# Pooled attention with a SoLU mixture layer on one core: the first four tiles' score maxima subtracted by TensorE, small scale steps merged, the order searched anew

## The chip, the cores and the metric

The kernel runs on one core of one Trainium2 chip, in one launch. The metric is device time in microseconds (us), as the median of the runs shown. The engines are called as in the profile: PE (TensorE; PEld is its weight load), DVE (VectorE), ACT (ScalarE), POOL (GpSimd) and SP, which here only issues DMAs.

## The reference

```python
def _attn_ref(q, k, v):                    # (8, 8, 576, 64) each
    k_p = k.reshape(B, H, 72, 8, D).mean(axis=3)
    v_p = v.reshape(B, H, 72, 8, D).mean(axis=3)
    scores = scale * np.matmul(q, k_p.transpose(0, 1, 3, 2))
    scores = scores - np.max(scores, axis=-1, keepdims=True)
    attn = np.exp(scores)
    attn = attn / (np.sum(attn, axis=-1, keepdims=True) + 1e-09)
    return np.matmul(attn, v_p)
def _moe_ref(x, w_in, w_out, g_ln):        # x (4608, 512), w_in (512, 1024), w_out (1024, 512)
    h = x @ w_in
    e = np.exp(h - np.max(h, axis=-1, keepdims=True))
    solu = h * (e / (np.sum(e, axis=-1, keepdims=True) + 1e-09))
    ln = (solu - mean(solu)) / np.sqrt(var(solu) + 1e-06) * g_ln
    return ln @ w_out
```

## The kernel before, in words

The 4,608 tokens are 36 tiles of 128. The batches go in pairs: four tiles of the even batch, one mixed tile that holds the last 64 tokens of both, four tiles of the odd batch. Each number that TensorE multiplies is held as two float16 parts, "hi" and "lo", so that a product takes three passes: hi by hi, hi by lo and lo by hi. The scale of such a pair is a power of two that is found on the chip: a maximum (`a_max`, L424), a spread over the partitions by PE (`a_par`, L470 and L480), a second maximum (`a_all`, L483) and three small DVE steps (`a_scale`, L489 to L499).

A tile goes through these steps (function, engine): `q_hi` ACT, `q_lo` DVE, a transpose of q by DMA (by PE for tile 0), `scores` PE, `s_max` DVE (L919), `s_sub` DVE (L922), `s_exp` ACT (L929), `e_sum`, `e_rec`, `e_mul` DVE, `e_hi` ACT, `e_lo` POOL, a transpose (by DMA; `e_Tp`, `e_Tc` by PE and ACT for tile 0), `av` PE (L998), `x_hi` ACT (L1007), `x_lo` DVE (L1011), `mm1` in three parts of 16 matmuls on PE (tile `hp`), `h_max`, `z_scale`, `z_mul` DVE, `h_exp`, `z_cen`, `z_hi`, `z_var` ACT, `z_lo` POOL, two transposes `z_T` by DMA, `mm2` in three parts on PE (tile `op`), `o_evac` ACT (L1150), `o_store`. Line 272 is the helper `mm`, which cuts a matmul with 128 weight columns into two with 64 each.

Ahead of the first `mm1` the weights are made ready. They arrive as 64-bit numbers, in four pieces of 1,024 KB for each matrix (wi 0 to 3, wo 0 to 3). `w_exp` and `w_sgn` (ACT), `w_shift` and `w_tail` (DVE) and `w_mul` (POOL) make float32 of a piece, `w_bnd` (PE), `w_rmax`, `w_all` and `wi_scale` or `wo_scale` (DVE, L704 and L756) its scale, `w_hi` (ACT, L788 and L791) the hi part, `w_res` (PE, L809 and L812) with `w_lo` (ACT, L823), or `w_lod` (DVE, L817), the lo part. K and V of batch 0 are pooled on PE with an identity in float32 (`pool_pe`, L405, evicted by `pool_ev`, L416), those of the others on POOL (`pool_kv`, L395).

Two things set the order. The buffers in PSUM: `ps_s` and `ps_x` have one buffer each (scores and K's transpose share the first, attention outputs, spreads and `v_rep` the second), `ps_h` has two (`hp`, the residues of the weights, PE's transposes). And the table `ORDER`: every operation has a number in it, the program emits them in that order, and each engine works off its queue in the order of these numbers; the durations and due times beside each `op` call do not enter the emitted program.

```python
    def op(eng, dur, t, fn, *args, r=(), w=(), u=(), after=()):
        ...
        ops.append((ORDER[name][count[name]], fn, args))
    ...
        for _, fn, args in sorted(ops, key=lambda o: o[0]):
            fn(*args)
```

By the table, PE's queue ahead of the first `mm1` ends with: `w_res` wo 1, `a_par` for K of batch 1, `e_Tp` 0, `v_rep` 0, `scores` 3, `w_res` wo 0, `av` 0. ACT's queue from `w_exp` wo 3 to the first `x_hi` holds three `w_hi` of wi among its work.

## Time and profile before

| | before |
|---|---|
| median of 3 runs | 493.37 us (492.62 to 495.02) |
| the profiled execution | 493.96 us |
| its span, first to last instruction | 492.2 us |
| PE busy | 464.2 us, 94% of the span |
| DVE busy | 371.7 us, 76% |
| ACT busy | 332.2 us, 67% |
| POOL busy | 305.8 us, 62% |
| DMA | 88.92 MB, mean 181 GB/s |

The profiled execution is 1.76 us longer than its span, and 0.59 us longer than the median. Times in the rows below are in us from the span's start. A busy share is a mean over stages that differ: the first 65 us hold no `mm1` at all, and in the last 20 us PE has only `mm2` left.

### The profile page before, as it was taken

The numbers are of one execution on the slowest core, as the hardware profiler recorded it, in microseconds if no ns is written. First come the engines' busy times: TensorE is split into PE (matmuls) and PEld (weight loads), VectorE is DVE, ScalarE is ACT, GpSimd is POOL, SyncE is SP. The second block draws the span as 40 slices with busy tenths as digits, with TensorE's granted clock in tenths as the row PEclk, the third lists the DMA queues.
The fourth block names the chain that finished last, engine by engine and source line by source line (L and its number), as shares of the span: only waits on it lengthen the run. The fifth ranks groups of instructions, "written<-read, shape, count | busy, mean of one in ns | idle before, by whom it ended". The sixth has DMA issues, their size and how long they took to land.

```text
span 492.2 us, 14712 instructions
## 1 busy us (share of the span) xinstructions
PE 464.2 (94%) x5976; PEld 301.0 (61%) x5976; DVE 371.7 (76%) x808; ACT 332.2 (67%) x521; POOL 305.8 (62%) x520
## 2 busy tenths in 40 slices
...
GB/s 301 359 309 197 160 103 188 182 215 165 216 213 216 201 217 128 247 178 209 189 174 166 179 200 204 188 143 174 212 215 171 114 156 125 116 102 136 55 117 87
DMA packets 197940, 88.92 MB, mean 181 GB/s; under 512 B 174312, under 2 KB 182512, under 8 KB 197360
## 3 DMA queue, kind: packets, MB, share of 16 engines
...
q14 instruction: 21, 0.17, 0.1%
...
## 4 chain that ended last, share of the span: by engine, by line
PE 63%; DVE 10%; POOL 10%; DMA 7%; ACT 4%; issue 3%; SPq 2%; POOLq 0%; ACTq 0%; DVEq 0%
PE op L272 27%; PE hp L272 26%; PE xp L998 4%; PE sc L272 3%; POOL vr L395 2%; DMA wir<-in_moe_w_in_dram 2%; DMA zT<-z 2%; DMA vr<-in_v_dram 2%; POOL kr L395 2%; POOL z L1092 2%; PE vrps L405 1%; DVE z L1072 1%; DVE m L1040 1%; POOL kp L395 1%; PE res_wo L809 1%
## 5 line engine op out<-in xcount | busy, mean ns | idle before, releaser
L272 PE MATMUL hp<-wi,xT 128*64 128x512 f16 x1728 | 197.7, 379 | 1.0 <-ACT xT L1007 0.9
L272 PE MATMUL op<-wo,zT 128*64 128x512 f16 x1728 | 197.7, 379 | 0.8 <-DMA zT<-z 0.6
L272 PEld LDWEIGHTS <-xT 128*64 128x64 f16 x1728 | 110.2, 110 | 70.4 <-ACT xT L1007 1.4
L272 PEld LDWEIGHTS <-zT 128*64 128x64 f16 x1728 | 111.3, 110 | 67.0 <-DMA zT<-z 1.1
L1092 POOL TENSOR_TENSOR z<-z,z 128x512 f16<-128x512 f32 x71 | 82.8, 1175 | 56.9 <-ACT z L1086 55.5
L1040 DVE TENSOR_REDUCE m<-hp 128x1 f32<-128x1024 f32 x36 | 43.9, 1218 | 27.1 <-PE hp L272 25.1
L977 POOL TENSOR_TENSOR e<-e,e 128x512 f16<-128x512 f32 x36 | 42.6, 1184 | 31.4 <-ACT e L969 31.3
L1051 ACT ACTIVATE z<-hp,nb,Hb 128x1024 f32<-128x1024 f32 x32 | 38.3, 1198 | 20.3 <-DVE nb L1043 18.4
L1072 DVE SCALAR_TENSOR_TENSOR z<-hp,rs,z 128x1024 f32<-128x1024 f32 x36 | 46.1, 1279 | 5.9 <-ACT z L1051 4.8
L1081 ACT ACTIVATE z<-z,sz 128x1024 f32<-128x1024 f32 x36 | 41.1, 1143 | 13.3 <-DVE z L1072 13.3
L1150 ACT ACTIVATE osb<-op,f 128x512 f32<-128x512 f32 x36 | 24.5, 680 | 29.5 <-PE op L272 23.9
L395 POOL TENSOR_TENSOR kr<-kr 128x512 f32<-128x512 f32 (+3 forms) x42 | 36.9, 886 | 9.3 <-DMA kr<-in_k_dram 8.6
L395 POOL TENSOR_TENSOR vr<-vr 128x512 f32<-128x512 f32 (+3 forms) x42 | 36.7, 878 | 5.7 <-DMA vr<-in_v_dram 3.7
L1086 ACT ACTIVATE z<-z 128x1024 f16<-128x1024 f32 x36 | 37.9, 1052 | 2.0 <-issue 1.4
L933 DVE TENSOR_REDUCE sc<-sc 128x8 f32<-128x576 f32 x36 | 27.4, 761 | 14.9 <-ACT sc L929 14.9
L1105 ACT ACTIVATE junk<-z 128x1024 f16<-128x1024 f32 x36 | 37.7, 1048 | 0.2
L919 DVE TENSOR_REDUCE mx<-sc 128x8 f32<-128x576 f32 x36 | 27.0, 750 | 10.7 <-PE sc L272 10.7
L998 PEld LDWEIGHTS <-vb 128*64 128x64 f16 x960 | 29.1, 111 | 7.0 <-DMA eT<-e 1.3
L998 PE MATMUL xp<-eT,vb 128*64 128x128 f16 (+1 forms) x960 | 31.1, 215 | 1.2 <-DMA eT<-e 0.9
L272 PEld LDWEIGHTS <-qT 128*64 128x64 f16 x1152 | 25.0, 114 | 9.0 <-issue 5.1
L272 PE MATMUL sc<-kT,qT 128*64 128x72 f16 x1152 | 25.9, 200 | 3.8 <-DVE e L948 2.7
L1011 DVE SCALAR_TENSOR_TENSOR xT<-xp,xT 128x512 f16<-128x512 f32 x36 | 24.6, 683 | 5.7 <-ACT xT L1007 5.5
...
## 6 DMA issues: line engine op xcount, KB each, us to landing
...
zT<-z SPq DMA_TRANSPOSE x72, 3.9
```

The source lines that it names most:

```text
L272: nc.tensor.matmul(out[lo : lo + 64] if m > 64 else out, lhsT=lhsT[:, lo : lo + 64], **kw)
L395: nc.gpsimd.tensor_tensor(out=dst, in0=src[:, :, :n], in1=src[:, :, n : 2 * n], op=ALU.add)
L933: nc.vector.tensor_reduce(out=tl[i]["r0"], in_=s_view(i), axis=AX.X, op=ALU.add)
L977: nc.gpsimd.tensor_tensor(out=e_main(i, 1), in0=e_src(i)[0], in1=e_main(i, 0), op=ALU.subtract)
L998: nc.tensor.matmul(xp[64 * e : 64 * e + 64, c, lo:hi], lhsT=vb[b % 2][:, n, c, e], rhs=eT[:, 2 * c + e if n < 2 else H + c // 2, lo:hi], s ...
L1040: nc.vector.tensor_reduce(out=small(i, "m"), in_=tl[i]["hp"], axis=AX.XY, op=ALU.max)
L1051: nc.scalar.activation(z, t["hp"], AF.Exp, bias=t["nb"], scale=hsc(i, 0), accum_out=small(i, "se"))
L1072: nc.vector.scalar_tensor_tensor(out=t["z"], in0=t["hp"], scalar=t["rs"], in1=t["z"], op0=ALU.mult, op1=ALU.mult, accum_out=small(i, "sz"),)
L1081: nc.scalar.activation(t["zf"], t["zf"], AF.Identity, bias=t["sz"], scale=-float(DFF))
L1086: nc.scalar.activation(t["z16"][:, 0], t["zf"], AF.Copy)
L1092: eng.tensor_tensor(out=t["z16"][:, 1, fs], in0=t["zf"][:, fs], in1=t["z16"][:, 0, fs], op=ALU.subtract)
L1105: nc.scalar.activation(junk, t["zf"], AF.Square, scale=DFF**-0.5, accum_out=small(i, "V"))
```

## The change

The change has four parts.

1. For tiles 0 to 3 `s_sub` is gone. In its place `s_psub` stands on PE: for each of the two banks it starts a new accumulation with a matmul of minus the identity (float32, `minus32`) by the maxima, spread over 288 columns, and adds all products of `scores` again on top of it.
2. The scale steps: `a_scale` has two steps instead of three (`a_unit`; the factor is moved into `identb`), `wi_scale` three DVE instructions instead of seven, `wo_scale` five instead of eight; the two steps for the norm's gain move to `g_all`, and two products move to POOL (`w_pwi`, `w_pwo`).
3. `idle` puts matmuls that compute nothing needed (128 by 128, float16) in front of five operations of PE: 46 ahead of its first `w_bnd`, 30 ahead of the first `a_par` for K, 19 ahead of the first `pool_pe` for V, 8 ahead of `q_Tp`, 4 ahead of `w_par` for wi: 107 in all.
4. `ORDER` is new throughout. Loads: wi 0 now goes ahead of K's first piece, and all of V's pieces go ahead of wo 3 (before, V's middle piece came last, behind wo 3). PE, ahead of the first `mm1`: `scores` 1, `w_bnd` wo 0 to 3, `s_psub` 1, `a_par` for V, `w_res` wi 1 and wi 0, `w_par` wo, `scores` 2, `w_res` wi 3, `s_psub` 2, `w_res` wo 1, `a_par` for K of batch 1, `e_Tp` 0, `v_rep` 0, `scores` 3, `w_res` wo 0, `av` 0, `s_psub` 3. DVE: `q_lo` 3 and `q_lo` 2 stand directly ahead of `a_all` and `a_unit` for V of batch 0. ACT: from `w_exp` wo 3 to the first `x_hi` the queue holds the same work with one `w_hi` of wi fewer, which is now ahead of `w_exp` wo 3; `s_exp` 1 is followed by `v_hi`; the second `e_hi` of tile 0 stands behind `w_hi` wo 1. At the end of the kernel PE's queue has `mm1` 34, `mm2` 33 and `mm2` 32 between `mm1` 35 and `mm2` 35 (before, `mm2` 31 too), and `mm2` 33, 32 and 35 between `mm1` 34 and `mm2` 34 (as before); SP's queue has tile 35's lo transpose ahead of its hi transpose, and POOL's has tile 34's `n_u` ahead of tile 35's `z_lo`.

```diff
@@ -20,212 +20,224 @@
 DEC = 2.0**-111
+IDLE = {
+    "a_par.k": {0: 30},
+    "pool_pe": {4: 19},
+    "q_Tp": {0: 8},
+    "w_bnd.wi": {0: 46},
+    "w_par.wi": {0: 4},
+}
 ORDER = {
...
 }
@@ -273,8 +285,8 @@
         nc.vector.tensor_scalar(
-            out=dst.bitcast(I32), in0=src.bitcast(I32), scalar1=EXPMASK, scalar2=None,
-            op0=ALU.bitwise_and,
+            out=dst.bitcast(I32), in0=src.bitcast(I32), scalar1=EXPMASK, scalar2=1 << 23,
+            op0=ALU.bitwise_and, op1=ALU.bitwise_or,
         )
@@ -307,7 +321,8 @@
     nc.scalar.activation(ident16, ident, AF.Copy)
-    nc.vector.tensor_copy(out=identb, in_=ident)
+    nc.scalar.activation(minus32, ident, AF.Copy, scale=-1.0)
+    nc.vector.tensor_scalar(out=identb, in0=ident, scalar1=1.0 / S14, scalar2=None, op0=ALU.mult)
     nc.gpsimd.memset(pmat4, 1.0)
@@ -332,6 +349,14 @@
+    todo_now = [None]
+    idle_at = {ORDER[nm][n]: c for nm, d in IDLE.items() for n, c in d.items()}
+    def idle(dst):
+        for _ in range(idle_at.get(todo_now[0], 0)):
+            nc.tensor.matmul(dst, lhsT=minus, rhs=minus, start=True, stop=True)
@@ -399,6 +424,7 @@
             bat[b][which + "ps"] = ps_h.tile([P, 2, 512], F32, tag="h", name=f"{which}ps{b}")
+        idle(bat[b][which + "ps"][:, 1, 384:])
         dst = bat[b][which + "ps"][:pp].rearrange("p a n -> p (a n)")[:, : NC * D]
@@ -486,14 +513,9 @@
-    def a_scale(nm, key, n):
+    def a_unit(nm, key, n):
         st = grp[nm, key]
         if n == 0:
-            nc.vector.tensor_scalar(
-                out=st["p"], in0=st["p"], scalar1=1e-30, scalar2=1.0 / S14, op0=ALU.max,
-                op1=ALU.mult,
-            )
-        elif n == 1:
             exp_bits(st["p"], st["p"])
@@ -696,24 +721,23 @@
-    def w_bound(nm):
+    def w_bound(nm, c):
         gm = wst[nm]["gm"]
-        nc.vector.tensor_scalar(out=gm, in0=gm, scalar1=2.0**-80, scalar2=None, op0=ALU.max)
+        nc.vector.tensor_scalar(
+            out=gm, in0=gm, scalar1=2.0**-80, scalar2=c, op0=ALU.max, op1=ALU.mult
+        )
         exp_bits(gm, gm)
...
     def wi_scale():
-        w_bound("wi")
-        nc.vector.tensor_scalar(
-            out=pwi, in0=wst["wi"]["gm"], scalar1=1.0 / S14, scalar2=None, op0=ALU.mult
-        )
+        w_bound("wi", 1.0 / S14)
         sw = const.tile([P, 1], F32, name="sw_wi")
-        nc.vector.reciprocal(out=sw, in_=pwi)
+        nc.vector.reciprocal(out=sw, in_=wst["wi"]["gm"])
         wst["wi"]["s"] = sw
-        for n, c in enumerate((2.0**-11, -(2.0**-11), 2.0**-7)):
-            nc.vector.tensor_scalar(
-                out=pw3[:, n : n + 1], in0=pwi, scalar1=c, scalar2=None, op0=ALU.mult
-            )
+    def w_pwi():
+        nc.gpsimd.tensor_scalar(
+            out=pw3, in0=c3, scalar1=wst["wi"]["gm"], scalar2=None, op0=ALU.mult
+        )
@@ -751,25 +775,27 @@
     def g_all():
-        wst["gm"] = all_max(wst["g"], "g")
-    def wo_scale():
-        w_bound("wo")
-        g2 = wst["gm"]
+        g2 = wst["gm"] = all_max(wst["g"], "g")
         nc.vector.tensor_scalar(out=g2, in0=g2, scalar1=1e-30, scalar2=None, op0=ALU.max)
...
+    def wo_scale():
+        w_bound("wo", 2.0**-13)
+        sg = const.tile([P, CO], F32, name="sg_wo")
+        nc.vector.tensor_tensor(
+            out=pw1, in0=wst["wo"]["gm"], in1=wst["gm"], op=ALU.mult
+        )
+        sw = const.tile([P, 1], F32, name="sw_wo")
+        nc.vector.reciprocal(out=sw, in_=pw1)
         nc.vector.tensor_scalar(
-            out=pwo, in0=g2, scalar1=wst["wo"]["gm"], scalar2=2.0**-13, op0=ALU.mult,
-            op1=ALU.mult,
-        )
-        sw = const.tile([P, 1], F32, name="sw_wo")
-        nc.vector.reciprocal(out=sw, in_=pwo)
-        nc.vector.tensor_scalar(
-            out=pwo, in0=pwo, scalar1=-(2.0**-8), scalar2=None, op0=ALU.mult
-        )
-        sg = const.tile([P, CO], F32, name="sg_wo")
-        nc.vector.tensor_scalar(out=sg, in0=g_sb, scalar1=sw, scalar2=None, op0=ALU.mult)
+            out=sg, in0=g_sb, scalar1=sw, scalar2=None, op0=ALU.mult
+        )
         wst["wo"]["s"] = sg
+    def w_pwo():
+        nc.gpsimd.tensor_scalar(
+            out=pwo, in0=pw1, scalar1=-(2.0**-8), scalar2=None, op0=ALU.mult
+        )
@@ -918,6 +947,20 @@
+    def s_psub(i):
+        mx = tl[i]["mx"].unsqueeze(3).to_broadcast([P, 2, HB, SP])
+        b, lo, hi = halves(i)[0]
+        for a in range(2):
+            mm(tl[i]["sc"][:, a, : HB * SP], lhsT=minus32, rhs=mx[:, a], start=True, stop=False)
+            for h in range(HB * a, HB * a + HB):
+                for x in range(2):
+                    mm(
+                        tl[i]["sc"][:, a, (h % HB) * SP : (h % HB + 1) * SP],
+                        lhsT=tl[i]["qT"][:, h],
+                        rhs=bat[b]["kT"][:, x, h * SP : (h + 1) * SP], start=False,
+                        stop=(h % HB == HB - 1 and x == 1),
+                    )
@@ -1166,6 +1210,7 @@
+    SUB_PE = (0, 1, 2, 3)
     TURN_Q, TURN_E, TURN_K = (0,), (0,), (0,)
@@ -1209,8 +1254,8 @@
                 w=[("p" + nm, key), ("s" + nm, key)])
-        for j in range(3):
-            n_ = op("dve", 0.16, t + 0.7 + 0.2 * j, a_scale, nm, key, j, u=[("p" + nm, key)],
+        for j in range(2):
+            n_ = op("dve", 0.16, t + 0.7 + 0.2 * j, a_unit, nm, key, j, u=[("p" + nm, key)],
                     w=[("s" + nm, key)], after=[n_])
@@ -1252,7 +1297,7 @@
         pool(b, "v", t)
-        op("pool", 0.35, t + 6.5, h_bat, b, r=[("sv", b), ("ws", "wi")], u=[("pv", b)],
+        op("pool", 0.35, t + 6.5, h_bat, b, r=[("sv", b), ("pw3",)], u=[("pv", b)],
            w=[("Hb", b)])
@@ -1317,14 +1362,16 @@
         if nm == "wi":
-            op("dve", 0.9, t_sum + 0.8, wi_scale, r=[("g2", nm)], w=[("ws", nm)])
+            op("dve", 0.5, t_sum + 0.8, wi_scale, r=[("g2", nm)], w=[("ws", nm)])
+            op("pool", 0.3, t_sum + 1.5, w_pwi, r=[("ws", nm)], w=[("pw3",)])
         else:
...
             op("dve", 0.28, t_sum - 2, g_all, r=[("x", "gg")], w=[("gg2",)])
-            op("dve", 1.2, t_sum + 0.8, wo_scale, r=[("g2", nm), ("gg2",)], w=[("ws", nm)])
+            op("dve", 0.5, t_sum + 0.8, wo_scale, r=[("g2", nm), ("gg2",)], w=[("ws", nm)])
+            op("pool", 0.3, t_sum + 1.5, w_pwo, r=[("ws", nm)], w=[("pwo",)])
         if nm == "wi" and any((nm, c) not in LO_DVE for c in range(4)):
@@ -1430,7 +1477,10 @@
         op("dve", 0.75, t(-2, 6.4), s_max, i, r=[("s", i)], w=K("mx"))
-        op("dve", 0.75, t(-2, 7.2), s_sub, i, r=K("mx"), w=[("s2", i)], u=[("s", i)])
+        if i in SUB_PE:
+            op("pe", 1.0, t(-2, 7.2), s_psub, i, r=K("mx", "qT") + [("kT", b) for b in bs], w=[("s2", i)], u=[("s", i)])
+        else:
+            op("dve", 0.75, t(-2, 7.2), s_sub, i, r=K("mx"), w=[("s2", i)], u=[("s", i)])
         op("act", 0.72, t(-2, 8.0), s_exp, i, r=[("s2", i), ("ct", key)], w=[("s3", i)], u=[("s", i)])
@@ -1482,7 +1532,7 @@
         op("pool", 1.1, t(1, 1.0), n_u, i, r=K("se", "pz"), w=K("u"))
-        op("pool", 1.1, t(1, 2.0), n_f, i, r=K("V", "u") + [("ws", "wo")], w=K("f"))
+        op("pool", 1.1, t(1, 2.0), n_f, i, r=K("V", "u") + [("pwo",)], w=K("f"))
         for c in range(3):
```

## Rows read from the trace of the kernel before

**Rows 1.** Busy time by stretch (us, count), granted clock, DMA share, GB/s.

```profile
65.35:488.03 422.68, 418.60 (x5554) 269.65 (x5554) 320.63 (x690) 285.91 (x456) 272.14 (x478) 1.00 0.87 171
36.60:64.70 28.10, 22.62 (x232) 11.54 (x230) 23.77 (x55) 23.25 (x37) 18.94 (x25) 0.94 0.67 159
40.30:65.35 25.05, 18.92 (x201) 9.05 (x200) 22.30 (x54) 20.57 (x36) 19.21 (x26) 0.93 0.69 168
66.00:100.00 34.00, 33.11 (x495) 20.11 (x493) 33.05 (x69) 28.19 (x46) 20.97 (x32) 1.00 0.92 173
```

**Rows 2.** Timeline of PE at the first mm1 (start, us, engine, line, operation).

```profile
62.59 1.06 PE L809 MATMUL res_wo<-wor,dg_wo 128*128 128x512 f32 x2
...
63.80 0.86 PE L998 MATMUL xp<-eT,vb 128*64 128x128 f16 x24
65.35 3.64 PE L272 MATMUL hp<-wi,xT 128*64 128x512 f16 x32 [0.69 <-ACT xT L1007]
```

**Rows 3.** Timeline of ACT, at wo 3 and at the first x_hi.

```profile
36.60 1.15 ACT L634 ACTIVATE u_wo<-wor 128x1024 f32<-128x1024 f32 x1 [1.66 <-DMA wor<-in_moe_w_out_dram]
...
64.70 0.60 ACT L1007 ACTIVATE xT<-xp 128x512 f16<-128x512 f32 x1 [0.64 <-PE xp L998]
```

**Rows 4.** Waits of ACT, 20 to 66 us (us in total, times, longest).

```profile
ACT vb L568 <- DVE sv L499: 2.7, 1, 2.7
```

**Rows 5.** Stretches of 2 us ahead of wo 3's landing.

```profile
30.00:32.00 2.00, 2.00 (x16) 1.98 (x17) 1.97 (x5) 2.00 (x4) 1.75 (x1) 1.00 1.02 412
32.00:34.00 2.00, 2.00 (x12) 2.00 (x10) 1.63 (x3) 2.00 (x4) 0.31 (x1) 1.00 1.05 323
```

**Rows 6.** Groups of DVE, 0 to 66 us.

```profile
L922 DVE TENSOR_TENSOR sc<-sc,mx 128x576 f32<-128x576 f32 x4 | 3.0, 761 | 0.1
```

**Rows 7.** Timeline of DVE: small scale steps, and q_lo twice.

```profile
29.50 0.26 DVE L713 TENSOR_SCALAR pw<-pwi 128x1 f32<-128x1 f32 x3
...
42.88 2.28 DVE L865 SCALAR_TENSOR_TENSOR q<-qr,sq('b', 0)_210,q 128x512 f16<-128x512 f32 x1
...
45.42 1.81 DVE L865 SCALAR_TENSOR_TENSOR q<-qr,sq('b', 0)_210,q 128x512 f16<-128x512 f32 x1
47.16 0.14 DVE L492 TENSOR_SCALAR pv<-pv 128x1 f32<-128x1 f32 x1
```

**Rows 8.** Timeline of PE: K's transpose, scores, residues of wi, small transposes.

```profile
24.60 2.39 PE L513 MATMUL kTp<-ident,kp 128*64 128x128 f32 x20
...
40.27 0.71 PE L272 MATMUL sc<-kT,qT 128*64 128x72 f16 x32
...
42.09 1.15 PE L809 MATMUL res_wi<-wo,dg_wi 128*128 128x512 f32 x2
...
43.29 1.06 PE L809 MATMUL res_wi<-wo,dg_wi 128*128 128x512 f32 x2
...
58.10 0.73 PE L882 MATMUL eTp<-ident,e 128*128 128x128 f16 x10
```

**Rows 9.** Waits of PE, 0 to 100 us.

```profile
PE gk L272 <- DVE amx_k L425: 2.4, 1, 2.4
```

**Rows 10.** Timeline of POOL at the slow q_lo, and of DVE at a later q_lo.

```profile
42.10 2.51 POOL L395 TENSOR_TENSOR kr<-kr 64x256 f32<-64x256 f32 x3
...
73.59 0.74 DVE L865 SCALAR_TENSOR_TENSOR q<-qr,sq('b', 1)_689,q 128x512 f16<-128x512 f32 x1
```

**Rows 11.** PE at a residue of wo, and the granted clock there.

```profile
55.62 1.91 PE L809 MATMUL res_wo<-wor,dg_wo 128*128 128x512 f32 x2
...
56.00:58.00 2.00, 2.00 (x5) 0.26 (x3) 1.36 (x4) 1.50 (x3) 1.26 (x1) 0.50 0.76 220
```

**Rows 12.** Timeline, 466 to 489 us: tile 34's chain at the end.

```profile
467.17 1.23 DVE L1040 TENSOR_REDUCE m<-hp 128x1 f32<-128x1024 f32 x1 [6.78 <-PE hp L272]
...
475.21 1.04 ACT L1086 ACTIVATE z<-z 128x1024 f16<-128x1024 f32 x1
```

**Rows 13.** The page, DMA issues: median us from issue to landing.

```profile
zT<-z SPq DMA_TRANSPOSE x72, 3.9
```

More of the change, by code (lines that the diff above doesn't have):

```diff
@@ L325 @@
     nc.gpsimd.memset(phalf, -0.5)
+    for n, c in enumerate((2.0**-11, -(2.0**-11), 2.0**-7)):
+        nc.gpsimd.memset(c3[:, n : n + 1], c)
     for t in vp:
@@ L471, in spread @@
         g = ps_x.tile([P, CI, P], F32, tag="x", name=name)
+        idle(g[:, CI - 1])
         for j in range(n):
@@ L509, in k_Tp @@
         bat[b]["kTp"] = tp
+        idle(tp[:, 896:])
         for c in range(NC):
@@ L597, in v_rep @@
         g = ps_x.tile([P, CI, P], F32, tag="x", name=f"vr{b}")
+        idle(g[:, CI - 1])
         bat[b]["vrep"] = g.rearrange("p c (e d) -> p c e d", e=2)
@@ L646, in w_bnd @@
             st["bnd"] = ps_o.tile([P, 512], F32, tag="o", name=f"bnd_{nm}")
+            idle(st["bnd"][:, 384:])
         bv = st["bnd"][:, :256].rearrange("p (j g) -> p j g", g=32)
@@ L807, in w_res @@
         wst[nm]["res", c] = t
+        idle(t[:, 1, 384:])
         for d in range(2):
```

331 lines of the change are left out of this document (171 added, 160 removed), and 90 rows, old and new, of the table ORDER.

## The prediction, made before the change was run

> **What bounds the kernel now.** I read the busy time by stretch first, then the timelines of PE and ACT around the first `mm1`, then what ACT waits for. The reader should see two stages. From 65.35 us, where the first `mm1` matmul starts, to 488.03, where the last eviction starts, PE is busy for 418.60 of 422.68 us [rows 1]: only 4.08 us are idle, and the work that PE has there is a fixed sum. So the end follows the start of the first `mm1`. Ahead of it no engine is full: from 40.30 to 65.35 DVE is busy for 22.30 of 25.05 us, ACT for 20.57, PE for 18.92 [rows 1]. The start hangs on a chain that changes hands: the last `w_res` of wo, `av` 0, `x_hi` 0, `mm1` [rows 2, 3]. ACT is the engine to follow, because everything it does after 36.60 stands in its queue behind `w_exp` wo 3, which had to wait for the last weight piece [rows 3]. From there to `x_hi` 0 at 64.70 it works for 23.25 us and waits for 4.85 [rows 1]; the longest wait, 2.7 us, is for V's scale [rows 4].
>
> **The change, part by part.** All queue positions are counted from the table and the calls; durations are from the profiled execution (493.96 us, span 492.2). It is 0.59 us above the median of 493.37, so I add the sum of the differences to the median.
>
> *After the first `mm1`.* None of the four `s_psub` and none of the 107 idle matmuls stands behind the first `mm1`, and `mm1`, `mm2`, `av`, `scores` and `v_rep` are as many as before. PE's work there changes by nothing. The end moves one for one with the start, and by what becomes of the 4.08 us of idle time.
>
> *`s_sub` for tiles 0 to 3.* DVE loses 4 x 0.76 = 3.0 us [rows 6]. PE gains four `s_psub`. Each is two float32 products over 288 columns, cut in two halves of 64 weight columns, and the 32 matmuls of `scores` again, 0.71 us [rows 8]. The trace has no such float32 product, so it is bounded. A residue step with 512 float32 and 512 float16 columns takes 43.29 - 42.09 = 1.20 us [rows 8], so 288 columns take at most 0.68; with the halves side by side that makes 2 x 0.68 + 0.71 = 2.05 us. K's transpose works in 64-wide float32 halves: 2.39 us for 8 x 128 + 2 x 64 = 1,152 columns [rows 8], 0.60 per 288, hence 4 x 0.60 + 0.71 = 3.1 us. Below, 1.4 us (the second `scores` twice over). I take 2.05, by the residue, since PE has as much to do around it as the residues have. A tile's score chain so grows by 2.05 - 0.76 = 1.3 us. For tiles 0 to 2 this lies beside ACT's other work, which has 7 us between `w_exp` wo 3 and `s_exp` 1. If that cover is gone, 1.3 us each come onto the path. PE's queue is in order: behind `s_psub` 1 wait V's `a_par` and two residues of wi, behind `s_psub` 2 a residue of wo, behind `s_psub` 3 the first `mm1`. The last is on the path: `s_psub` 3 stands between `av` 0 and `mm1` 0, where `x_hi` now fills 65.35 - 64.70 = 0.65 us [rows 2, 3]. It adds 2.05 - 0.65 = 1.4 us, bounds 0.7 and 2.5.
>
> *Scale steps.* A small DVE step costs 0.14 us, or 0.09 in a row of three [rows 7]. Gone ahead of the first `mm1` are one for each of three scales, four for wi and one for wo (two more of wo only move): 9 x 0.14 = 1.3 us at most, of which 0.6 lie behind wo 3. POOL gets two of them; `w_pwi` stands ahead of `h_bat` 0 and `e_lo` 0 in its queue and waits for nothing late. Together with three `s_sub` (2.3) DVE has 2.9 us less to do in the 25.05 us ahead of the start, 19.4 instead of 22.3 [rows 1]: DVE is then no reason for a start later than 40.3 + 19.4 = 59.7, as long as it does not wait.
>
> *Idle matmuls.* Ten 128-column transposes take 0.73 us [rows 8], 0.073 each, twice that at half the clock; 46 take 3.4 to 6.7 us, at the very start, where PE has nothing loaded yet; 30 take 2.2 to 4.4, where PE waited 2.4 us for K's maximum [rows 9]. The rest stand where PE waits for loads. I cost them at nothing: the cover is the loads. Without it, up to 2 us come onto K's chain, which ends long ahead of ACT's. I give them no gain either, as the path starts with wo 3.
>
> *The loads.* SP's queue puts all of V ahead of wo 3, so one more piece of 0.52 MB lands before it. At the mean of 412 and 323 GB/s [rows 5] this is 1.4 us: wo 3 lands at 38.0 instead of 36.60 (bounds 36.6 and 39.4). V, in return, is ready before it is asked for.
>
> *ACT from there.* One `w_hi` of wi, 1.2 us, has moved ahead of wo 3; the rest is the same, 23.25 - 1.2 = 22.05 us. Of the 4.85 us of waits the 2.7 for V's scale should go, because `a_unit` now follows `a_all` directly and no `s_sub` stands before it. What is late next is `x_hi`'s own wait for `av` (0.64 [rows 3]) and some wait for PE's residues: I take 1.6 us in all, bounds 0.6 and 4.85.
>
> *The sum.* 38.0 + 22.05 + 1.6 = 61.65 for `x_hi`, + 0.65 + 1.4 = 63.7 for the first `mm1`: 1.65 us earlier. The low ends give 36.6 + 22.05 + 0.6 + 0.65 + 0.7 = 60.6, the high ends 39.4 + 22.05 + 4.85 + 0.65 + 2.5 = 69.4. Behind the start, DVE is busy for 33.05 of 34 us up to 100 us [rows 1]; it enters that stage with more lead, and I let 0.5 of the 4.08 us of idle time go (bounds 2 less, 2 more, since all positions are new). At the end tile 35's hi transpose now stands behind its lo one. A tile's chain takes 8.0 us from `h_max` to `z_hi` [rows 12], 1.04 for it and 3.9 for the transpose [rows 13], 13 us; three triples of parts (48 matmuls each, at 3.64 us for 32 [rows 2]) cover 16, so the new place costs 0 to 1 us; I take 0. In all -1.65 - 0.5 = -2.15, so 493.37 - 2.15 = **491.2 us**.
>
> **The rivals.** *The order gains more.* If ACT waits little and the halves of `s_psub` overlap, the start moves towards 60.6, 4.75 us earlier, which gives 488.6, or 486.6 with 2 us of idle time gone. For it speaks that no engine is full ahead of the start; against it, that ACT, DVE and PE must then all run nearly without a wait.
>
> *DVE waits for POOL.* `q_lo` took 2.28 and 1.81 us where POOL added beside it, and 0.74 where it did not [rows 7, 10]. In the new order both of these `q_lo` stand directly ahead of V's `a_all`, at about the time of POOL's `w_mul` of wo 2 and of its first sums for K. If they wait as before, V's scale comes 1.54 + 1.07 = 2.6 us later, ACT waits for it again, and the start is 63.7 + 2.6 = 66.3: 493.8 to 494.3, no change. The Trainium skill (SBUF — State Buffer, section "SBUF: two separate sides") says that VectorE and GpSimd share a pair of ports as an exclusive lock, held for a whole instruction. By that rule the two waits return wherever POOL starts first; the rows agree with it, as 2.28 is about POOL's 2.51 us. For it: the rows. Against: POOL may be waiting for K's loads just then.
>
> *Slower: the second scores at the lower clock.* Between 56 and 58 us the granted clock was 0.50, that is 1.2 instead of 2.4 GHz, and a residue pair took 1.91 us instead of 1.06 [rows 2, 11]. `s_psub` 2 and 3 are placed in that stage. At the lower level each takes 4.1 us or more, and both are ahead of the first `mm1` in PE's own queue: 63.7 + 4.1 = 67.8, so 495.8, and with the float32 halves one after the other 2.1 more, 497.9. It decides once the two cost over 4.6 us more than I took. Against it: the new order fills PE with residues and `s_psub` there.
>
> **How the numbers follow.** The forecast (489.9 to 492.5) gets 0.40, of which 0.17 is below 490.9; more gain (486.5 to 489.9) 0.24; no change by POOL (492.5 to 495) 0.20; slower (495.8 to 498) 0.16. Half a per cent, 2.5 us, is about what can be told from no change here: faster is below 490.9, slower above 495.8. Faster 0.24 + 0.17 = 0.41, same 0.23 + 0.20 = 0.43, slower 0.16. The range from 487.3 to 496.4 leaves out some 0.05 below and 0.12 above.
>
> **What would show it.** Right: the first `mm1` starts near 63.7; from there to the last eviction it takes about 422 us again; wo 3 lands near 38; ACT's wait for V's scale is gone; an `s_psub` takes about 2 us, and the one of tile 3 ends where the first `mm1` begins. Wrong: a start that has not moved although DVE has 3 us less to do; `q_lo` again at 2 us; a granted clock of 0.50 under `s_psub`; or idle time of PE behind the start that differs from 4 us by more than 2, which would put the cause into the order of the later tiles.

## The result, and the profile after

The changed kernel takes **498.57 us** as the median of 4 runs (497.83 to 500.59), against 493.72 for the kernel before (4 runs beside it): a ratio of **1.0117**, interval 1.0083 to 1.0151. It is slower by 1.2%. Its profiled execution took 497.88 us, 3.92 more than that of before (493.96).

Two stretches of the changed kernel in the busy time by stretch (as in [rows 1]): from the first `mm1` to the last eviction, and from `w_exp` wo 3 to `x_hi` 0; then five stretches of 2 us.

```profile
68.25:491.97 423.72, 419.50 (x5566) 272.57 (x5558) 325.68 (x678) 286.63 (x456) 274.45 (x480) 1.00 0.88 170
40.93:66.94 26.01, 24.21 (x307) 12.78 (x307) 19.26 (x45) 22.01 (x36) 18.03 (x23) 0.95 0.86 177
30.00:32.00 2.00, 1.61 (x45) 1.21 (x42) 1.05 (x8) 1.35 (x2) 2.00 (x2) 1.00 1.08 217
32.00:34.00 2.00, 1.40 (x28) 0.86 (x26) 1.97 (x3) 2.00 (x3) 0.93 (x1) 1.00 1.03 193
34.00:36.00 2.00, 1.61 (x36) 1.31 (x30) 0.74 (x1) 2.00 (x5) 0.79 (x1) 1.00 1.03 172
40.00:42.00 2.00, 2.00 (x8) 1.55 (x8) 0.00 (x0) 1.07 (x2) 0.00 (x0) 0.50 0.34 78
98.00:100.00 2.00, 2.00 (x34) 1.41 (x31) 1.92 (x4) 0.23 (x1) 1.50 (x2) 0.50 1.16 247
```

ACT's timeline, at the places that answer to [rows 3] and at its longest wait between them:

```profile
40.93 1.12 ACT L658 ACTIVATE u_wo<-wor 128x1024 f32<-128x1024 f32 x1 [3.25 <-DMA wor<-in_moe_w_out_dram]
...
55.28 0.69 ACT L828 ACTIVATE dg_wo<-ident,sg_wo 128x128 f32<-128x128 f32 x2 [1.65 <-DVE sg_wo L790]
...
66.94 0.60 ACT L1051 ACTIVATE xT<-xp 128x512 f16<-128x512 f32 x1 [1.03 <-PE xp L1042]
```

PE's timeline: V's last part, `scores` 2, `av` 0, `s_psub` 3 and the first `mm1` (as in [rows 2]); then `av` 4, behind the start, with what comes after it.

```profile
38.71 2.71 PE L431 MATMUL vrps<-vr,ident 128*128 128x128 f32 x16 [3.10 <-DMA vr<-in_v_dram]
...
54.71 0.71 PE L284 MATMUL sc<-kT,qT 128*64 128x72 f16 x32 [1.80 <-DMA qT<-q]
...
66.04 0.86 PE L1042 MATMUL xp<-eT,vb 128*64 128x128 f16 x24
66.73 0.66 PE L284 MATMUL sc<-mx,minus 128*64 128x288 f32 x4
67.22 0.42 PE L284 MATMUL sc<-kT,qT 128*64 128x72 f16 x16
67.48 0.68 PE L284 MATMUL sc<-mx,minus 128*64 128x288 f32 x4
68.00 0.42 PE L284 MATMUL sc<-kT,qT 128*64 128x72 f16 x16
68.25 3.62 PE L284 MATMUL hp<-wi,xT 128*64 128x512 f16 x32
...
96.64 0.95 PE L1042 MATMUL xp<-eT,vb 128*64 128x64 f16 x48 [1.84 <-DVE xT L1055]
97.71 1.06 PE L284 MATMUL sc<-kT,qT 128*64 128x72 f16 x32
98.52 3.29 PE L284 MATMUL op<-wo,zT 128*64 128x512 f16 x16
```

**Where 3.92 us came from.** The first `mm1` starts at 68.25 instead of 65.35: +2.90. What follows (execution time less that start) takes 429.63 instead of 428.61: +1.02. Counted along ACT's queue, the 2.90 are four differences: wo 3 lands at 40.93 instead of 36.60 (+4.33); from there to `x_hi` 0 ACT works 22.01 us instead of 23.25 (-1.24) and waits 4.00 instead of 4.85 (-0.85); from `x_hi` 0 to `mm1` it is 1.31 instead of 0.65 (+0.66), because `s_psub` 3 stands between. While V's pieces and the end of wo were under way, from 30 to 36 us, the DMAs moved 172 to 217 GB/s, where those of before had moved 412 and 323 in the first four of these microseconds [rows 5].

**The chain that set the start.** This sum says what ACT did, not what the start hung on. The profile's chain of work that ended last (start, us, what), followed back from the end, does not pass through ACT or wo 3's `w_exp` in this stretch. It goes from the load of V's last piece over its pooling, the residues of wi, `scores` 1, `s_max` 1 and the two `q_lo` to the transposed load of q (tile `qT`) for `scores` 2:

```profile
25.42 13.15 DMA vr<-in_v_dram
...
38.71 2.71 PE vrps L431 x16
41.42 1.71 PE res_wi L836 x2
...
44.59 0.66 PE sc L284 x32
...
45.28 0.76 DVE mx L948
...
47.00 1.32 DVE q L892 x2
...
48.39 6.27 DMA qT<-q
```

PE stands 3.10 us at the head of its queue for this piece of V. Its granted clock is then 0.50 from 40 to 42 us, the pooling takes 2.71 us (2.02 in e7 below, at the full clock), and `scores` 1 starts at 44.52 instead of 40.27 [rows 8]. `scores` 2 waits 1.80 us for its q. From there to the first `mm1` PE has no idle time left; these are the stretches of the changed kernel and of the kernel before:

```profile
54.71:68.25 13.54, 13.54 (x214) 7.62 (x216) 12.62 (x29) 11.09 (x20) 9.84 (x16) 1.00 0.69 143
52.49:65.35 12.86, 9.91 (x128) 5.00 (x127) 11.60 (x29) 11.19 (x19) 8.13 (x14) 0.87 0.51 118
```

What PE has more to do there are two second passes (3.0 us) and a residue step of wi (2.4 us). ACT's waits for `s_exp` 2 and for `av` 0 are waits for PE.

Behind the start PE waits 1.84 us for `x_lo` 3, and after that wait the granted clock is 0.50 from 98 to 100 us, that is 1.2 GHz: 16 matmuls of `mm2` take 3.29 us where at 87.73 and 92.91 us they took 1.89.

### The profile page after: what moved, and what is told of

The parts are those of the page before. It is cut to its first block, busy times and chain, and to the rows that moved or that the text cites. A ratio compares the mean times of both kernels' runs of the same rounds, so it can differ in the third digit from the quotient of the medians.

```text
span 496.2 us, 15231 instructions
## 1 busy us (share of the span) xinstructions
PE 471.9 (95%) x6243; PEld 310.6 (63%) x6243; DVE 374.2 (75%) x783; ACT 333.6 (67%) x522; POOL 308.0 (62%) x525
## 4 chain that ended last, share of the span: by engine, by line
PE 65%; DVE 12%; DMA 10%; ACT 4%; POOL 4%; issue 3%; SPq 1%; ACTq 0%; POOLq 0%; DVEq 0%
PE op L284 29%; PE hp L284 26%; DMA vr<-in_v_dram 4%; PE xp L1042 4%; PE sc L284 3%; DMA wor<-in_moe_w_out_dram 3%; DVE q L892 2%; DVE z L1116 2%; DVE m L1084 1%; DMA qT<-q 1%; DMA eT<-e 1%; DVE sc L965 1%; DVE mx L948 1%; DMA wo<-in_moe_w_in_dram 1%; POOL z L1136 1%
## 5 line engine op out<-in xcount | busy, mean ns | idle before, releaser
L284 PEld LDWEIGHTS <-xT 128*64 128x64 f16 x1728 | 111.5, 110 | 68.2 <-ACT xT L1051 0.5
L1051 ACT ACTIVATE xT<-xp 128x512 f16<-128x512 f32 x36 | 21.3, 591 | 26.9 <-PE xp L1042 26.7
L284 PEld LDWEIGHTS <-qT 128*64 128x64 f16 x1280 | 28.1, 113 | 9.8 <-issue 2.5
```

The lines of the kernel that those rows point to most:

```text
L284: nc.tensor.matmul(out[lo : lo + 64] if m > 64 else out, lhsT=lhsT[:, lo : lo + 64], **kw)
```

## The experiments

"Start" is the first `mm1` in the profiled execution, "rest" the time of that execution less the start. The medians are over 4 to 12 executions. Each ratio is against executions of the kernel before taken beside that run (their medians were 492.97 to 494.69), so it is not the quotient of the medians shown. A profile is one execution, and not always one near the median: those of e6, e8, e9, e11, e13 and e17 were the fastest of their run, those of e2, e10, e14 and e15 the slowest.

| run | what | median, us | ratio to before (interval) | start | rest |
|---|---|---|---|---|---|
| | before | 493.72 | | 65.35 | 428.61 |
| | changed | 498.57 | 1.0117 (1.0083 to 1.0151) | 68.25 | 429.63 |
| e17 | changed, again | 498.75 | 1.0134 (1.0094 to 1.0174) | 68.64 | 427.99 |
| e6 | before, V ahead of wo 3 | 496.03 | 1.0043 (1.0004 to 1.0083) | 66.00 | 427.67 |
| e7 | changed, V behind wo 3 | 496.19 | 1.0048 (1.0012 to 1.0085) | 65.39 | 430.39 |
| e2 | the same, V pooled late | 499.25 | 1.0130 (1.0092 to 1.0168) | 72.58 | 429.56 |
| e1 | changed, `x_lo` 3 earlier | 499.81 | 1.0142 (1.0106 to 1.0179) | 68.79 | 429.52 |
| e3 | e1 and e2 | 499.90 | 1.0150 (1.0109 to 1.0190) | 69.65 | 429.97 |
| e9 | e7, all of `av` 4 earlier | 495.73 | 1.0063 (1.0037 to 1.0089) | 65.14 | 428.67 |
| e16 | e9, `w_lod` first | 497.19 | 1.0065 (1.0033 to 1.0098) | 67.73 | 432.02 |
| e18 | e9, K's loads of before | 497.46 | 1.0094 (1.0063 to 1.0126) | 67.98 | 428.69 |
| e4 | changed, `s_sub` on DVE | 506.06 | 1.0265 (1.0235 to 1.0295) | 72.88 | 433.18 |
| e8 | e4 with idle matmuls | 505.33 | 1.0229 (1.0193 to 1.0266) | 68.60 | 434.30 |
| e5 | before, `s_psub` on PE | 505.47 | 1.0234 (1.0200 to 1.0269) | 74.72 | 430.58 |
| e10 | e9, tile 3 on DVE, late | 500.19 | 1.0144 (1.0109 to 1.0180) | 66.11 | 435.37 |
| e13 | e9, tile 3 on DVE, early | 497.72 | 1.0098 (1.0061 to 1.0135) | 65.11 | 432.32 |
| e14 | e9, tiles 2, 3 on DVE, early | 497.45 | 1.0107 (1.0061 to 1.0153) | 66.35 | 432.62 |
| e15 | e9, all four on DVE, early | 499.61 | 1.0121 (1.0071 to 1.0171) | 67.30 | 432.95 |
| e11 | changed, no idle matmuls | 499.50 | 1.0129 (1.0092 to 1.0166) | 65.11 | 431.85 |
| e12 | before, scale steps merged | 494.72 | 1.0042 (1.0017 to 1.0067) | 63.82 | 429.40 |

### The place of V's last load (e6, e7, e2, e3, e17)

In the table of before, e6 moves one entry:

```diff
-"load_kv": vr 1 at 102 (wo 3 at 101)
+"load_kv": vr 1 at 100
```

> The kernel before with one load moved: the last part of V (0.52 MB) ahead of the last piece of wo instead of behind it, as the changed kernel has it. Theory (a 64-partition piece of V goes at some 200 GB/s, so it costs 2.6 us and not 1.4): wo 3 lands 2.5 to 3.5 us later, at 39 to 40 us, and as ACT's wait for V's scale shrinks by about 1.5, the first mm1 is 1 to 2.5 us later, 494.5 to 496. Rival (the prediction's price, at the mean rate): wo 3 at 38.0, ACT's wait for V's scale gone, the first mm1 no later than before, 492 to 493.5.

ACT's and PE's timelines of e6, wo 3 and the first `mm1`:

```profile
38.81 1.12 ACT L640 ACTIVATE u_wo<-wor 128x1024 f32<-128x1024 f32 x1 [3.24 <-DMA wor<-in_moe_w_out_dram]
...
66.00 3.64 PE L278 MATMUL hp<-wi,xT 128*64 128x512 f16 x32 [0.69 <-ACT xT L1013]
```

wo 3 lands 2.2 us later than in [rows 3], not 1.4: 0.52 MB in 2.2 us are some 240 GB/s. The start moves by 0.65 only, and the time by 0.4% (ratio 1.0043). The landing is nearer to the theory's 2.5 us than to the prediction's 1.4; the start is under the theory's 1 to 2.5 us and not, as the rival has it, at or under that of before. PE does not wait for V here.

e7 goes the other way, in the changed kernel:

```diff
-"load_kv": vr 0 at 96      "pool_pe": vr 0 at 97
+"load_kv": vr 0 at 103.5   "pool_pe": vr 0 at 108.5   (wo 3 at 103, scores 1 at 109)
```

> The changed kernel with V's part 0 loaded behind the last piece of wo, and its pooling on PE at place 108.5, ahead of scores 1 (in the run before it stood behind scores 1, whose own transposed load then came later). Theory (the place of the piece of V only decides which of two waits comes last, since all of V and wo must land before V's scale and the last weights are ready): wo 3 at 38 to 39 us, V's pooling at 41 to 42.5, the first mm1 at 66.5 to 68.5, 496.5 to 498.5. Rival (wo 3 alone sets the start): the first mm1 at 65 to 66, 494.5 to 496.

ACT's and PE's timelines of e7:

```profile
37.71 1.15 ACT L665 ACTIVATE u_wo<-wor 128x1024 f32<-128x1024 f32 x1 [0.33 <-DMA wor<-in_moe_w_out_dram]
...
39.20 2.02 PE L438 MATMUL vrps<-vr,ident 128*128 128x128 f32 x16 [1.45 <-DMA vr<-in_v_dram]
41.15 0.71 PE L291 MATMUL sc<-kT,qT 128*64 128x72 f16 x32
...
65.39 3.62 PE L291 MATMUL hp<-wi,xT 128*64 128x512 f16 x32
...
93.79 0.95 PE L1049 MATMUL xp<-eT,vb 128*64 128x64 f16 x48 [1.95 <-DVE xT L1062]
```

wo 3 is 3.2 us earlier and the start 2.9 earlier: my theory fell, and the rival's start came. The ratio fell from 1.0117 and 1.0134 to 1.0048, which is 3.4 to 4.2 us of about 6. The wait at `av` 4 is untouched. With V's piece behind wo 3 the stretch that had moved 217 GB/s moves 406:

```profile
30.00:32.00 2.00, 1.51 (x42) 1.01 (x38) 1.33 (x8) 1.67 (x2) 2.00 (x2) 1.00 1.03 406
```

That wo 3 alone sets the start is not shown by this. The edit moves two things, the load and the pooling, and the pooling now stands behind a residue step of wi on PE. PE works on that step instead of waiting 3.10 us for V, then waits 1.45; its clock stays at 1.00 there, and `scores` 1 starts at 41.15 instead of 44.52, though V's piece lands later than in the changed kernel. No run moves only one of the two in this order. And e9 and e16 below, which have e7's order up to the start, have wo 3 at 38.91 and 38.39 and the start at 65.14 and 67.73.

e2 had been the first try. It left V's pooling on PE at a place behind `scores` 1:

```diff
+"load_kv": vr 0 at 103.5   "pool_pe": vr 0 at 113.5
```

> The changed kernel with V's part 0 (0.52 MB) loaded behind the last piece of wo, not ahead of it, and its pooling on PE moved back accordingly. Theory (the piece of V is what makes the last piece of wo late): wo 3 lands at 36.5 to 37.5 us instead of 40.9, the first mm1 starts 2 to 3.5 us earlier, at 64.8 to 66.3, and the time is 495 to 496.5. Rival (V's maximum and scale are the next thing late: part 0 then lands at about 41 and ACT waits for V's scale instead): wo 3 is early, the first mm1 stays at 67.5 or later, 497.5 to 498.6.

In its waits `scores` 1 stands 4.9 us for its transposed q, V's pooling behind it in PE's queue, and ACT 8.3 us for the pooled V; the start went to 72.58 although wo 3 was early (38.81). One place in PE's queue was worth 7 us of the start in these two profiles, with the load in the same place. e3 is e2 with e1's move below:

> Both of the two moves before at once. Theory (two separate losses, one ahead of the first mm1 and one behind): they add up to 5 to 7 us, 491.5 to 493.5 us, which is at or a little under the kernel before (493.7). Rival (DVE's lead at the start of the main stage is what both take from): together they give no more than the larger of the two, 494.5 to 496.

It shows the same wait (ACT 6.0 us for V) and no gain; as a test of whether the two add up it says nothing.

> The changed kernel as it is, once more, so that it and the mended ones stand against the same runs of the kernel before, and so that its loads are seen in a second profile. Theory (wo 3 lands late whenever V's part stands ahead of it): wo 3 at 40 to 41.5 us again and the first mm1 at 67.5 to 69; 497.5 to 499.5, a ratio of 1.009 to 1.013. Rival (the late landing was that one run's: the changed kernel without idle matmuls had it at 38.4 with the same loads): wo 3 below 39 us, the first mm1 at 65 to 66.5 in this profile, though the median over the runs stays where it is.

```profile
40.39 1.13 ACT L658 ACTIVATE u_wo<-wor 128x1024 f32<-128x1024 f32 x1 [2.78 <-DMA wor<-in_moe_w_out_dram]
...
68.64 3.62 PE L284 MATMUL hp<-wi,xT 128*64 128x512 f16 x32
...
97.05 0.95 PE L1042 MATMUL xp<-eT,vb 128*64 128x64 f16 x48 [1.82 <-DVE xT L1055]
```

These rows of the unchanged changed kernel, ACT and PE, show the late landing and the wait at `av` 4 a second time, here without the fall of the clock behind the start. So the late landing is no accident of one profile, though e11, with the same loads, had it at 38.41. PE waits 2.71 us for V again, and its clock is at 0.50 from 38 to 44 us.

### The wait behind the start (e1, e9, e16)

e1 moves `x_lo` 3 from place 359 to 343.5.

> The changed kernel with one step moved: the low half of x for tile 3 (x_lo 3) stands at DVE's place 343.5 instead of 359, so the single PSUM buffer that av 4 waits for comes free earlier. Theory (the new order left this one step late, and PE's wait then also lowers its clock): the wait of 1.84 us ahead of av 4 at 96.6 us and the slow op and sc groups behind it go; from the first mm1 to the last eviction it takes about 420 us instead of 423.4; 494.5 to 495.5 us, 3 to 4 us under the changed kernel's 498.6. Rival (DVE is behind by as much as it has too much work, so the wait only moves to the next step): the first wait goes, another of over 1 us appears by 130 us, and the time stays at 497.5 to 498.6.

PE's and DVE's timelines of e1:

```profile
97.99 0.85 PE L1048 MATMUL xp<-eT,vb 128*64 128x64 f16 x24 [2.38 <-DVE vb L603]
...
94.24 2.64 DVE L898 SCALAR_TENSOR_TENSOR q<-qr,sq('b', 1)_983,q 128x512 f16<-128x512 f32 x1
```

The rival's second wait came, though the time (499.81) is above what either had said. `av` 4 now waits 2.38 us for the other thing that it needs, the second `v_x`, which stands behind `q_lo` 8; where two releasers are late, a profile names only the last. e9 therefore moves all three, with e7's loads:

```diff
+"x_lo": 3 at 343.5   "v_x": 343.6 and 343.7 (from 350 and 355)
```

> The changed kernel with V's part 0 loaded behind the last piece of wo (pooled ahead of scores 1), and on VectorE x_lo 3 and the two v_x of the next batch moved to 343.5 to 343.7, ahead of w_lod wo 2, q_lo 8 and e_sum 5: all that av 4 waits for, not x_lo alone. Theory (the wait at 94 us was for the last of two things, x_lo 3 and v_x 1 0, both behind q_lo 8; the move of x_lo alone left the other): the first mm1 at 65 to 66, no wait of PE over 1 us between 85 and 105, no granted clock below 0.95 behind the first mm1, 492 to 493.5. Rival (VectorE has too much to do in this stretch, so the wait moves to the mm2 that needs w_lod or to q_T 8): a wait of 1.5 us or more by 130 us, 495 to 496.5.

PE's waits in e9 from 65 to 490 us:

```profile
PE sc L293 <- DVE e L1000: 1.7, 2, 1.3
PE op L293 <- DVE wo L853: 1.6, 1, 1.6
```

The wait at `av` 4 is down to 0.6 us at most and the low clock behind the start is gone, but the `mm2` that needs `w_lod` and the `scores` that wait for `e_mul` now wait. The ratio, 1.0063, does not differ from e7's by what can be told. e16 puts `w_lod` back ahead of the second `v_x`:

> The run with the loads and av 4's three steps moved, with w_lod wo 2 and the first v_x left ahead of the second v_x (x_lo 3 at 343.5, the second v_x at 350.5). Theory (that run's wait of 1.6 us of mm2 for w_lod was made by the move): no wait of PE for w_lod, av 4 starts at most 0.7 us later, 494 to 495.5. Rival (VectorE has too much to do here in any order): the waits behind the start add to the same 2 to 4 us, 495.5 to 496.5.

The wait for `w_lod` is gone, that for `e_mul` is 2.8 us, and the ratio is 1.0065. Between the three orders (e7, e9, e16) no difference can be told. DVE is busy for 32.9 to 33.4 of the 34 us up to 100 us in all three, as in [rows 1]; that each order only chooses who waits is how I read this.

This profile of e16, one of its slower executions (499.75), shows something else: up to the start its order is that of e9, and yet the start is 2.6 us later. PE's timeline at `scores` 2, first of e9, then of e16:

```profile
51.60 0.71 PE L293 MATMUL sc<-kT,qT 128*64 128x72 f16 x32 [0.91 <-DMA qT<-q]
...
52.60 0.71 PE L293 MATMUL sc<-kT,qT 128*64 128x72 f16 x32 [1.97 <-DMA qT<-q]
```

In e16 q's transposed load is later, and the granted clock falls to 0.52 from 54 to 56 us. So the start differs between executions of one order by nearly as much as the moved load had brought.

### The subtraction itself (e4, e8, e5, e10, e13 to e15)

e4 gives the four subtractions back to DVE (`SUB_PE = ()`), each `s_sub` at the place of its `s_psub`.

> The changed kernel with the maxima of tiles 0 to 3 subtracted by VectorE again, at the same places of the order; everything else as changed. Theory (the second scores cost little: only the pass of tile 3 stands on the path, some 0.7 to 1.1 us ahead of the first mm1, against 0.76 us for each of the four on DVE): the first mm1 at 67.5 to 68.5 us and the time at 497 to 499. Rival (TensorE's four passes of 1.5 us are what makes the start late): the first mm1 at 64 to 66 and the time at 494 to 496.5.

It was slower still, by 7 us: both theories missed. The busy time by stretch of e4, in two low stretches:

```profile
38.00:40.00 2.00, 1.56 (x7) 1.59 (x8) 1.97 (x3) 0.33 (x1) 0.00 (x0) 0.50 0.30 44
66.00:68.00 2.00, 2.00 (x31) 1.37 (x28) 1.35 (x3) 2.00 (x5) 1.25 (x2) 0.50 0.27 52
```

The granted clock is at 0.50 from 34 to 42 us (0.52 up to 44) and again from 66 to 70. e8 puts 20 idle matmuls where each `s_psub` had been, and `s_sub` behind them:

```diff
+def s_fill(i):
+    for _ in range(20):
+        nc.tensor.matmul(tl[i]["sc"][:, 1, 384:], lhsT=minus, rhs=minus, start=True, stop=True)
```

> The changed kernel with VectorE subtracting the maxima of tiles 0 to 3, and TensorE doing 20 idle 128-column matmuls where the second passes of scores stood (their results are not used). Theory (the second passes held TensorE's clock up; without them it fell to half, and that made the run without them 6 to 7 us slower): the stretches at granted clock 0.50 at 34 to 44 and 64 to 71 us shrink to what the changed kernel has, and the time is 498 to 501. Rival (VectorE's 3 us are what counts, the clock only follows its waits): the low stretches stay in large part and the time is 504 to 507.

The same stretches of e8:

```profile
38.00:40.00 2.00, 1.98 (x9) 2.00 (x10) 1.97 (x3) 0.00 (x0) 0.00 (x0) 0.50 0.28 34
66.00:68.00 2.00, 2.00 (x37) 1.32 (x36) 1.96 (x8) 0.98 (x3) 2.00 (x4) 1.00 0.50 92
```

The clock holds at 66 to 70 and is at 0.50 from 38 to 40 in place of 34 to 42, and the start is back at 68.60, 4.3 us ahead of e4. Yet the rest is 434.30, with PE waiting 2.3 us for `x_hi` and 2.2 for `x_lo`, and the median did not move (505.33 against 506.06). So the clock is the likely cause of e4's late start, from one profile of each, but it is not what made the kernel slow: the rival's time came, though its low stretches did not stay.

e5 asks the reverse, `s_psub` in the order of before (`SUB_PE = (0, 1, 2, 3)`, `ORDER["s_psub"] = ORDER["s_sub"][:4]`).

> The kernel before, in its own order, with the maxima of tiles 0 to 3 subtracted by TensorE's second pass at the places where VectorE's subtraction stood. Theory (the second pass by itself costs little; the new order is what made the kernel slower): the first mm1 0.5 to 1.5 us later than the 65.35 us of before, 494 to 495. Rival (the second pass is the cause of the slower kernel): first mm1 at 67.5 or later, 496.5 to 498.5. Second rival (it keeps TensorE busy and so its clock up, as its removal from the changed kernel lowered it): the stretch at granted clock 0.50 at 54 to 58 us is gone and the first mm1 is at 63.5 to 65, 491.5 to 493.

PE's timeline of e5:

```profile
63.30 0.71 PE L274 MATMUL sc<-kT,qT 128*64 128x72 f16 x32 [1.53 <-DVE e L966]
67.02 1.23 PE L274 MATMUL sc<-mx,minus 128*64 128x288 f32 x4 [3.01 <-DVE mx L923]
...
70.15 1.76 PE L813 MATMUL res_wo<-wor,dg_wo 128*128 128x512 f32 x2
...
74.72 3.64 PE L274 MATMUL hp<-wi,xT 128*64 128x512 f16 x32 [0.69 <-ACT xT L1025]
```

The first mm1 starts 9.4 us later. This is the prediction's slow rival, in the old order: `s_psub` 3 waits 3.01 us for its maxima at the head of PE's queue, a residue and `av` 0 stand behind it, the clock is at 0.50 from 66 to 70 us, and the pass itself takes 3.1 us (67.02 to 70.15) instead of 1.5. The subtraction on PE needs an order made for it, and e4 shows that this order in turn does not suit DVE's.

Then places that suit DVE. e10 is e9 with `s_sub` 3 at 235, the place of `s_psub` 3:

> The kernel of the run before, with the maxima of tile 3 subtracted by VectorE and those of tiles 0 to 2 by TensorE. Theory (from 51 us on TensorE has hardly an idle stretch, so each second pass there costs its 1.5 us, and VectorE's 0.76 us for it is cheaper if it has the lead): first mm1 0.7 to 1.5 us earlier, 491 to 492.5. Rival (VectorE has no lead to give, as the two runs with its subtraction in all four tiles showed): start earlier all the same, but new waits of PE for VectorE behind it, 494 to 496.5.

ACT's and PE's timelines of e10:

```profile
69.84 0.71 ACT L982 ACTIVATE sc<-sc,ct('b', 0)_422 128x576 f32<-128x576 f32 x1 [3.06 <-DVE sc L975]
...
75.84 3.19 PE L294 MATMUL hp<-wi,xT 128*64 128x512 f16 x16 [2.36 <-ACT xT L1061]
```

The place was wrong: `s_sub` 3 stood behind `k_lo` and `w_tail`, ACT's `s_exp` 3 waited 3.06 us, and `x_hi` 1 behind it was late. e13, e14 and e15 put one, two and all four directly behind their `s_max` (218.3; 172.3; 77.3 and 114.3).

> As the run of tile 3's subtraction on VectorE, but directly behind that tile's s_max (place 218.3) and not at 235, where it waited behind three longer steps and held ACT for 3.06 us. Theory (the second pass of tile 3 is 1.5 us on a TensorE that has no idle stretch there, against 0.76 us on VectorE): the first mm1 0.7 to 1.5 us ahead of the run with all four on TensorE (495.7), no long wait of ACT for s_sub, 494 to 495.2. Rival (VectorE has no lead to give): new waits of TensorE for it behind the start, 496 to 499.

> The same with tiles 2 and 3 on VectorE, each directly behind its s_max. Theory: the second passes of tiles 2 and 3 are 3 us of TensorE's time in a stretch where it does not idle, so the first mm1 comes 1.5 to 2.5 us earlier than with all four on TensorE, 493 to 494.5. Rival (VectorE has no lead): 496 to 499.

> The same with all four on VectorE, each directly behind its s_max: the subtraction of before in the changed order, at places that suit it. Theory (the second pass is a loss of its own, apart from the order): 492.5 to 494.5, at or under the kernel before. Rival (the order needs TensorE's passes, as they hold its clock and spare VectorE 3 us): low clock again between 32 and 44 us and waits of TensorE for VectorE behind the start, 499 to 506.

The medians are 497.72, 497.45 and 499.61, none under e9's 495.73. In their profiles the rest is 432.3 to 433.0 against 428.7, and the start is no earlier. So at these places nothing speaks for the theory that the second passes are a loss of their own. They may be a gain of up to 3 us in this order, but the intervals of e15 and e9 overlap, and e16, with all passes on PE, has a rest of 432.0 too; e9's profile is the fastest of its twelve executions.

### Idle matmuls, scale steps, K's loads (e11, e12, e18)

e11 is the changed kernel with an empty `IDLE`.

> The changed kernel without its 107 idle matmuls. Theory (they lie in waits for loads and hold the clock there): the clock falls in one more stretch ahead of 40 us, the first mm1 within 1 us of 68.25, 498 to 500. Rival (they stand in front of K's chain and cost up to 2 us): the first mm1 1 to 2 us earlier, 496.5 to 497.5.

The granted clock is 0.50 in the slices from 16 to 26 us, in the changed kernel's profile from 14 to 18, and falls again at 50 and 94 us. The start of this one profile is early (65.11, with wo 3 at 38.41), the median is that of the changed kernel: the idle matmuls cost and give nothing that can be told.

e12 is the kernel before with `a_unit`, `wi_scale`, `wo_scale`, `w_pwi` and `w_pwo` as changed, and its own order.

> The kernel before with the merged scale steps alone, in the order of before. Theory (nine small steps of 0.14 us gone from VectorE ahead of the first mm1, 0.6 us of them behind wo 3): the first mm1 0 to 1 us earlier, 492.5 to 494.5. Rival (the two steps given to POOL come late there, and their readers wait): the first mm1 later by 1 us or more, 495 to 497.

The profiled execution has its start at 63.82, 1.5 us earlier, in line with the prediction's merit for them, and took 493.22. The median of 10 runs is nevertheless 0.4% above before. Where the other runs lose it, this profile can't show.

e18 gives e9 the kernel before's places for K's parts 0 and 2 (-1 and 10).

> The run with the loads and av 4's three steps moved, with K's first and last part also loaded where the kernel before had them (part 0 at the very start, part 2 behind wi 1). Theory (K's chain ends well ahead of the chain from wo 3, so it changes nothing): the first mm1 within 0.7 us, 495 to 496.5. Rival (scores 0, which the new order starts at 31 us instead of 28.7, sets what follows, the rest that is still open): scores 0 1.5 to 2.5 us earlier, and with them the first mm1, 493 to 494.5.

`scores` 0 starts at 31.52, as without it (31.74 in e9), the ratio is 1.0094, and the start is later: `scores` 2 waits 2.64 us for q's transposed load. Neither theory's time came out, and nothing says that K's loads are what is missing.

## Why the prediction was wrong

Predicted were 491.2 us with a range of 487.3 to 496.4; measured were 498.57.

- **The path: the step that failed.** I took ACT as "the engine to follow" and wrote that ahead of the start "no engine is full" and that V "is ready before it is asked for", without a price for the opposite. PE waited 3.10 us for V's last piece at the head of its queue, at the lower clock behind it, and 1.80 us for q's transposed load, and from `scores` 2 on it was busy for 13.54 of 13.54 us. The chain of the changed kernel runs there, and my sum has it only as "some wait for PE's residues" among ACT's 1.6 us. That the landing, too, was late does not decide: with wo 3 between 37.71 and 38.91 the start was at 65.39 (e7), 65.14 (e9), 67.73 (e16), and, with V pooled later still, 69.65 (e3) and 72.58 (e2).
- **wo 3's landing: the term that was too small.** "At the mean of 412 and 323 GB/s this is 1.4 us: wo 3 lands at 38.0 (bounds 36.6 and 39.4)." It landed at 40.93 and 40.39, outside the bounds. I took the rate from stretches in which the weights move [rows 5]. V's piece costs 2.2 us in e6 and about 3 between e7 and the changed kernel. It comes as two transfers of 64 partitions each. The rows to read had been there, in the busy time by stretch of the kernel before, where V's first pieces land (issued at 13.16 us, with a median of 12.6 from issue to landing); the last number is GB/s:

```profile
22.00:24.00 2.00, 1.23 (x16) 0.86 (x12) 2.00 (x4) 2.00 (x3) 0.34 (x1) 1.00 1.07 208
24.00:26.00 2.00, 1.73 (x22) 1.69 (x24) 2.00 (x4) 2.00 (x3) 0.00 (x0) 1.00 1.11 226
```

  The Trainium skill (DMA: Bandwidth & Descriptors, section "🎯 Rules for kernel authors") advises one 128-partition transfer over two to disjoint halves, as the two serialize; the 172 to 226 GB/s here are in line with it, though no run here loads V in one transfer. With V behind wo 3 the landing is 37.71 in e7, 38.91 in e9 and 38.39 in e16, where my sum without the piece would have said 36.6. So another 1.1 to 2.3 us do not come from the place of that piece, and no run shows from what.
- **ACT from there.** The work was right: 22.05 us predicted, 22.01 measured. The wait for V's scale went, as said, from 2.7 [rows 4] to 0.4 (1.6 in e17). But the waits were 4.00, not 1.6, within their bounds: what came late next was wo's scale (1.65, DVE behind a spread that waits in PE's queue), `s_exp` 2 (0.85) and `av` (1.03). They are 4.32 in e7, 2.95 in e9 and 6.05 in e16, with the same work: between executions of one order they differ by 3 us. I had counted the wait that goes and guessed the next one from what the old trace showed.
- **`s_psub`.** Priced at 2.05 us with bounds 1.4 and 3.1; it takes 1.5 at the full clock, near the low bound, and 3.1 at the half. As the last step ahead of `mm1` it costs 0.66 instead of 1.4. Counted along ACT, four terms make up the miss of the start: 68.25 - 63.7 = 4.55 = 2.93 (landing) - 0.04 (work) + 2.40 (waits) - 0.74 (`s_psub` 3).
- **Behind the start.** I let 0.5 us of idle time go; the profiled rest grew by 1.02, within the bounds of 2. The reason to look for was named (an order in which all positions are new, DVE full), the place was not: `av` 4. Its mending gave nothing that can be told; DVE has 0.6 to 1.1 us free of 34 there in three orders.
- **The rivals.** DVE behind POOL, where I put it, did not occur in the changed kernel's first profile, where `q_lo` 3 and 2 took 1.40 us together; in its second (e17) they took 2.64, in e7 3.08 and in e16 2.99, ahead of q's transposed load. It occurs elsewhere too; `q_lo` 8 took 2.64 us in e1. That 2.28 us "is about POOL's 2.51" set one step of DVE against three of POOL [rows 10]. The slow rival, `s_psub` at the lower clock, did not occur in the changed kernel (its `s_psub` ran at the full clock), but it is what happens in the old order (e5). Its price of 4.1 us for one pass was too high (3.1), and the 3.01 us that it waits there at the head of PE's queue had no price at all.
- **The scale steps.** One for each of three scales, four for wi and one for wo are eight, 1.1 us, where I wrote nine. It enters no term of the sum.
- **The tail** was right: `mm2` of the last tiles runs without a stall.

What is shown: V's load behind wo 3, together with its pooling behind a residue step, returns 3.4 to 4.2 us of about 6 (the ratios of e7 against those of the changed kernel; with further moves on top, e9, e16 and e18 returned 1.1 to 3.5). How much of it is wo 3's landing and how much PE's wait for V is not shown; in the old order the load's place alone cost 0.4% (e6). The late `x_lo` 3 costs nothing that can be told. What stays open is the remaining half per cent. No gain came from moving the subtraction back (e13 to e15), K's loads (e18) or the wait at `av` 4 (e9, e16). e9's profiled execution (493.81) equals that of before, and yet its median is 0.6% above; that profile was the fastest of twelve, which go up to 500.79. One thing that e16's and e18's profiles show and no run tests is the wait of `scores` 2 for q's transposed load, 1.97 and 2.64 us; in the kernel before `scores` 2 waits 1.01 us, for DVE. The merged scale steps alone measured 0.4% slower in the old order (e12), which is of the size that is missing, but no row shows how. No version beat the kernel before.
